# A decode step of attention and an MLP: engine programs written on their own semaphores, with each token's head outputs placed once

## The chip, the cores and the metric

The kernel runs on one core of a Trainium2 chip. A core has five engines that run their own instruction streams: TensorE (PE; its weight loads are listed as PEld), VectorE (DVE), ScalarE (ACT), GpSimd (POOL) and SyncE (SP), and 16 DMA engines that move data between the device memory and the on-chip memory SBUF. Engines wait for each other on semaphores. The metric is the device time in microseconds; lower is better.

## The reference, cut to what matters

Two tokens (B = 2) go through a layer norm; attention reads a cache of 8192 keys and values for each of 32 heads; an MLP makes a gate.

```python
xn = _layernorm(x)                                    # (2, 1, 512)
q = (xn @ wq).reshape(B, 1, 32, 128)                  # and heads in front
scores = einsum("bhqd,bhkd->bhqk", q, k_cache) * 128 ** -0.5
p = softmax(scores)
o = einsum("bhqk,bhkd->bhqd", p, v_cache)
s = o.reshape(B, 1, 4096) @ wo                        # (2, 1, 512)
g = silu(gelu(_layernorm(xn) @ w1 + b1) @ w2 + b2)
return x + s * g
```

All data are float32. Each of `k_cache` and `v_cache` has 268 MB; `wq` and `wo` have 8.4 MB each, `w1` and `w2` 2.8 MB each. Every byte is read once.

## The kernel before

The work is written in Bass under the Tile framework, which hands out buffers and sets the semaphores; the order of each engine's instructions is written out by hand (`manual_schedule`).

Two heads (U = 2) of one token make a turn; there are N = 32 turns, 16 for each token. In a turn one tile of keys and one of values, 8.4 MB each, is loaded. A tile lies with 64 of its rows (partitions) for each head, and 128 keys of 128 elements in each row. SP issues all the large loads. There are two buffers for keys (`kpool`) and one for values (`vpool`); at the start the key buffers hold `wq` and the first keys, and the value buffer (`boot`) the weights and small tensors of the MLP; at the end `wo` takes the value buffer.

Before the loop: layer norms, the MLP with its gate (`mlp`), then `project_q`, which makes the queries of all heads. `queries(k)` spreads four turns' queries over the partitions, with two products on PE and a copy on ACT; it is called once before the loop and then in every fourth turn.

In turn n the loop at L393 puts down:

- `scores_mul` (L317): DVE multiplies the keys by the query, in two halves, in place;
- between the halves `max_dve` (L335) and `exps` of the turn before: the negated maximum of each head goes through PE (L346) and ACT (L348) to all partitions, ACT makes the exponentials (L354) in `PZ` and their sums, and puts the sums in `ZR` (L357);
- `weighted` of the turn before (L369): 32 products of `PZ` with the values add up in `po`, each on one of four groups of 32 partitions; PE spends two instructions on each float32 product;
- `load_v(n)`, which needs the value buffer and so those products at their end;
- `scores_sum` (L322): DVE sums the products over the 128 elements; `max_rows` (L326) and the transposition `max_pe` (L330);
- `place` of the turn before, and `load_k(n + 2)`, which needs the key buffer that this turn has read. In the turn before the last, the last values are loaded into a key buffer, in halves.

Two turns make a group (G = 2). They share `po`; there are two of those and two `PZ`. In the second turn of a group `weighted` copies `po` to SBUF (L375) and four products turn it (L378) so that the elements lie along the partitions; `place` spreads the result on DVE over a window of `Z` (L386), and a product with a shifted view of `Z` adds it to `OA` at the rows of these heads (L390). The sums go the same way, from `ZR` (L360). `OA` is set to zero by a product at the start (L162).

After the loop, `wo` is loaded in five pieces as soon as the value buffer is free (L67), the last turn's products follow, DVE divides `OA` by the sums (L435, L437), PE multiplies by the pieces of `wo` (L442, L451, L456), DVE applies the gate (L459, L460), and two small DMAs write the output (L463). At L486 the framework ends the program: SP waits on the semaphores, the engines drain and meet, POOL clears the semaphores, and the engines meet again.

Of the kernel before, what the change touches and what calls it, by code (L numbers as in the profile page):

```python
# [1 line left out]

# [16 lines left out]
@with_exitstack  # L19
def decode_kernel(ctx: ExitStack, tc: tile.TileContext, x, kc, vc, wq, wo, w1, b1, w2, b2, out):  # L20
    nc = tc.nc
# [10 lines left out]
    G = 2  # L32
# [10 lines left out]
    ZP = P - G * UP  # L43
# [8 lines left out]
    consts = ctx.enter_context(tc.tile_pool(name="consts", bufs=1))  # L52
    kpool = ctx.enter_context(tc.tile_pool(name="kpool", bufs=2))
    vpool = ctx.enter_context(tc.tile_pool(name="vpool", bufs=1))
    small = ctx.enter_context(tc.tile_pool(name="small", bufs=2))
    ps_c = ctx.enter_context(tc.tile_pool(name="ps_c", bufs=1, space=bass.MemoryType.PSUM))
    ps_s = ctx.enter_context(tc.tile_pool(name="ps_s", bufs=4, space=bass.MemoryType.PSUM))
    ctx.enter_context(tc.manual_schedule())


    K, V = {}, {}
    kf = kc.rearrange("b h s d -> (b h s d)").rearrange("(n p j d) -> n p j d", p=P, j=KP, d=DH)
    vf = vc.rearrange("b h s d -> (b h s d)").rearrange("(n p j d) -> n p j d", p=P, j=KP, d=DH)

    def load(dst, src, cuts):
        for a, e in zip(cuts, cuts[1:]):
            nc.sync.dma_start(dst[:, a:e], src[:, a:e])  # L67

    def load_k(n, cuts=(0, KP)):
        K[n] = kpool.tile([P, KP, DH], F32, tag="k", name=f"k{n}")  # L70
        load(K[n], kf[n], cuts)

    def load_v(n, cuts=(0, KP), pool=vpool, tag="v"):
        V[n] = pool.tile([P, KP, DH], F32, tag=tag, name=f"v{n}")
        load(V[n], vf[n], cuts)

    HALVES = (0, KP // 2, KP)
# [5 lines left out]
    wq_sb = kpool.tile([P, ND, H * DH], F32, tag="k", name="wq_sb")  # L83
    boot = vpool.tile([P, KP * DH], F32, tag="v", name="boot")
    used = [0]

    def take(p, n, base=0, at=None):

        if at is None:
            at = used[0]  # L90
            used[0] += n
            assert used[0] <= KP * DH
        return boot[base:base + p, at:at + n]

    w1_sb = take(P, ND * F).rearrange("p (c f) -> p c f", f=F)
    w2_sb = take(P, WB * P)

    at = used[0]
    take(P, F + D)
    x_sb, xn, y = (take(B, D, 0, at + D * i) for i in range(3))  # L100
    b1_sb = take(1, F, R, at)
    b2_sb = take(1, D, R, at + F)
    h_row = take(B, WR * P, 2 * R, at).rearrange("b (r p) -> b r p", p=P)
    h_nat = take(B, WB * R + WM * (QT - 1), 3 * R, at)
    hs = take(P, WM * QT * QT * B).rearrange("p (a c j b) -> p a c j b", c=QT, j=QT, b=B)
    fold = take(P, QT * P).rearrange("p (c m) -> p c m", m=P)
    g_sb = take(P, 512)
    z = take(P, P)
    th = take(P, P)


    nc.sync.dma_start(w1_sb, w1.rearrange("(p c) f -> p c f", p=P))
    nc.sync.dma_start(w2_sb, w2.rearrange("f n -> (f n)").rearrange("(p e) -> p e", p=P))
    nc.sync.dma_start(wq_sb, wq.rearrange("(p c) n -> p c n", p=P))
    load_k(0, HALVES)


    eps_t = consts.tile([B, 1], F32, name="eps_t")
    nc.vector.memset(eps_t, EPS)
    warm = small.tile([B, 1], F32, tag="warm", name="warm", bufs=1)  # L120
    nc.scalar.activation(warm, eps_t, AF.Sqrt)
    nc.scalar.dma_start(x_sb, x.rearrange("b s d -> (b s) d"))
    for t, src in ((b1_sb, b1), (b2_sb, b2)):
        nc.scalar.dma_start(t.rearrange("o (k e) -> o k e", k=16), src.rearrange("(o k e) -> o k e", o=1, k=16))


    ident = consts.tile([P, P], F32, name="ident")
    make_identity(nc, ident)
    ones = consts.tile([P, B], F32, name="ones")
    nc.vector.memset(ones, 1.0)  # L130
    srow = consts.tile([1, P], F32, name="srow")
    nc.vector.memset(srow, SCALE)

    mod = consts.tile([P, R], F32, name="mod")

    blk = consts.tile([P, QT], F32, name="blk")

    cls = take(P, QT)

    half = consts.tile([P, UP], F32, name="half")  # L140
    nc.vector.memset(half, 0.0)
    for s in range(U):
        nc.vector.memset(half[HP * s:HP * (s + 1), PH * s:PH * (s + 1)], 1.0)

    Z = consts.tile([P, P + ZP], F32, name="Z")
    ZR = consts.tile([P, P + ZP], F32, name="ZR")
    nc.gpsimd.memset(Z, 0.0)
    nc.gpsimd.memset(ZR, 0.0)


    PZ = [consts.tile([P, NT, G, U, JW], F32, name=f"pz{n}") for n in range(G)]
    for t in PZ:
        nc.gpsimd.memset(t, 0.0)

    PO = [ps_c.tile([P, JW * DH], F32, name=f"po{n}") for n in range(2)]
    acc = ps_c.tile([P, P], F32, name="acc")
    OA = ps_c.tile([P, B, OC + 1], F32, name="OA")
    for t in PO + [acc]:
        nc.vector.memset(t, 0.0)

    zeros = PZ[0].rearrange("p t g s j -> p (t g s j)")
    nc.tensor.matmul(OA.rearrange("p b c -> p (b c)"), zeros[:, :P], zeros[:, :B * (OC + 1)],  # L162
                     start=True, stop=False)


    def layernorm(dst, src):
        st = take(B, nc.vector.BN_STATS_DIM)
        nc.vector.bn_stats(st, src)
        mv = take(B, nc.vector.BN_AGGR_DIM)
        nc.vector.bn_aggr(mv, st)  # L170
        sd = take(B, 2)
        nc.scalar.activation(sd[:, 0:1], mv[:, 1:2], AF.Sqrt, bias=eps_t, scale=1.0)
        nc.vector.reciprocal(sd[:, 1:2], sd[:, 0:1])
        nc.vector.tensor_scalar(dst, src, mv[:, 0:1], sd[:, 1:2], op0=ALU.subtract, op1=ALU.mult)

    def transposed(to, src, name):

        p = ps_s.tile([P, P], F32, tag="s", name=f"pt_{name}")
        for c in range(ND):
            nc.tensor.transpose(p[:, c * B:(c + 1) * B], src[:, c::ND], ident[:B, :B])  # L180
        nc.scalar.copy(to, p[:, :ND * B].rearrange("p (c b) -> p c b", b=B))


    x4 = consts.tile([P, P], F32, name="x4")
    px = ps_s.tile([P, P], F32, tag="s", name="px")
    nc.vector.memset(px, 0.0)
    for j in range(QT):
        nc.tensor.matmul(px[R * j:R * j + B, :], ident[:B, :B], x_sb[:, j * P:(j + 1) * P], start=True, stop=True)
    nc.scalar.copy(x4, px)

    layernorm(xn, x_sb)
    by_row = ident.rearrange("p (j r) -> p r j", r=R)
    nc.vector.tensor_reduce(out=mod, in_=by_row, axis=AX.X, op=ALU.add)
    nc.vector.tensor_reduce(out=blk, in_=ident.rearrange("p (j r) -> p j r", r=R), axis=AX.X, op=ALU.add)
    layernorm(y, xn)

    xnT = take(P, ND * (2 * NQ - 1) * B).rearrange("p (c b) -> p c b", c=ND)
    nc.vector.memset(xnT, 0.0)
    transposed(xnT[:, :, (NQ - 1) * B:NQ * B], xn, "xn")
    yT = take(P, ND * B).rearrange("p (c b) -> p c b", b=B)  # L200
    transposed(yT, y, "y")


    gate = consts.tile([P, P], F32, name="gate")
    for m in range(QT):
        nc.vector.tensor_reduce(out=cls[:, QT - 1 - m:QT - m], in_=ident[:, m::QT], axis=AX.X, op=ALU.add)
    nc.vector.memset(h_nat, 0.0)
    nc.gpsimd.memset(fold, 0.0)
    nc.vector.tensor_copy(fold.rearrange("p c (j r) -> p c j r", r=R)[:, :, :, :B],
                          mod.rearrange("p (c j b) -> p c j b", j=QT, b=B))  # L210

    def mlp():

        for f in range(0, F, 512):
            w = min(512, F - f)
            ph = ps_s.tile([P, 512], F32, tag="s", name=f"ph{f}")
            for c in range(ND):
                nc.tensor.matmul(ph[:B, :w], yT[:, c, :], w1_sb[:, c, f:f + w], start=(c == 0), stop=False)  # L218
            nc.tensor.matmul(ph[:B, :w], ones[R:R + 1, :B], b1_sb[:, f:f + w], start=False, stop=True)  # L219
            nc.scalar.copy(h_nat[:, 1 + f:1 + f + w], ph[:B, :w])  # L220

        for m in range(QT):
            nc.vector.tensor_copy(  # L223
                h_row[:, :, m::QT],
                h_nat[:, WM * m:WM * m + WB * R].rearrange("b (k e) -> b e k", e=WB)[:, :WR, :])
        ph = ps_s.tile([P, P], F32, tag="s", name="ph")
        for r in range(WR):
            nc.tensor.transpose(ph[:, r * B:(r + 1) * B], h_row[:, r, :], ident[2 * R:2 * R + B, 2 * R:2 * R + B])  # L228

# [46 lines left out]
    def project_q():  # L276
# [11 lines left out]
        nc.scalar.copy(q_nat, p)  # L288

    Q = {}  # L290

    def queries(k):

        b, e = divmod(k, HH // NB)
# [196 lines left out]
```

## Time and profile before

| | |
|---|---|
| median of 3 runs | 1305.62 us (1305.46 to 1305.83) |
| the profiled execution | 1305.79 us |
| its span, first to last instruction | 1303.8 us |
| DVE busy | 1132.3 us |
| PE busy | 408.2 us |
| ACT busy | 68.4 us |
| moved by DMA | 559.67 MB, 429 GB/s over the span |

The page divides the span into 40 slices and gives, for each engine and for the DMA engines, the busy share of a slice in tenths. The chain of work that ended last is followed back from the last instruction, at each step to what released it. In the timeline, a row has the start in us, the duration in us, the engine (with a `q` for the engine's queue, where it issues a DMA), the line, the operation and the tensors, how many instructions stand in the row, and in brackets how long the engine was idle before and what ended that.

### The profile page before, as it was taken

The page shows a single profiled execution, that of the slowest core. Times are in us where ns is not written, and L with a number is a line of the kernel's source. Part 1 is how long each engine was busy: PE and PEld are TensorE (multiplying, and loading weights), DVE is VectorE, ACT ScalarE, POOL GpSimd, SP SyncE. Part 2 cuts the span into 40 slices and gives each one's busy share as a digit, 9 for nine tenths or more (in the row PEclk, how much of TensorE's full clock was granted, in tenths as well). Part 3 has the DMA queues.
Part 4 walks back from the last instruction along what each step waited for, and adds up shares of the span by engine and source line. Part 5 has one row for each costly group of instructions (what it writes and reads, how often), then busy time and mean ns, then how long its engine had stood idle before and what let it go on. Part 6 is the DMA issues. An engine that isn't in the chain of part 4 may idle for free.

```text
span 1303.8 us, 6086 instructions
## 1 busy us (share of the span) xinstructions
PE 408.2 (31%) x2638; PEld 128.0 (10%) x2638; DVE 1132.3 (87%) x258; ACT 68.4 (5%) x234; POOL 2.6 (0%) x11
## 2 busy tenths in 40 slices
PE   5312333312233321323321333321323332233326
PEld 1100101001010100101000010100101010010102
DVE  3599989988889988888988888988888998888990
ACT  1000000000000000000000000000000000000000
POOL 0000000000000000000000000000000000000000
PEclk9756666556666655666655666655666665666667
DMA  9999999999999999999999999999999999999997
GB/s 409 439 420 445 424 443 426 439 426 441 424 439 426 441 426 433 434 433 436 429 438 430 431 431 434 433 433 434 431 436 431 437 424 443 424 438 429 432 426 321
DMA packets 10849, 559.67 MB, mean 429 GB/s; under 512 B 1212, under 2 KB 1220, under 8 KB 1480
## 3 DMA queue, kind: packets, MB, share of 16 engines
q1 hardware_dynamic: 10808, 559.29, 99.3%
q8 instruction: 20, 0.33, 0.1%
q14 instruction: 5, 0.04, 0.0%
q10 hardware_dynamic: 16, 0.01, 0.0%
HBM read 559.30 MB, written 0.00 MB: 429 GB/s over the span
## 4 chain that ended last, share of the span: by engine, by line
DMA 75%; PE 24%; issue 0%; ACT 0%; DVE 0%; SPq 0%
DMA v<-in_A_v_cache_dram 72%; PE po L369 22%; DMA wo_sb<-in_A_wo_dram 2%; PE ph L218 1%; DMA boot<-in_B_w_dram 1%; PE po L284 1%; PE pw L252 0%; PE po L442 0%; PE ph L219 0%; DVE boot L223 0%; PE acc L451 0%; ACT L236 0%; PE pgate L258 0%; PE ph L228 0%; SPq L67 0%
## 5 line engine op out<-in xcount | busy, mean ns | idle before, releaser
L317 DVE TENSOR_TENSOR k<-k,q 128x8192 f32<-128x8192 f32 x64 | 555.6, 8681 | 112.6 <-DMA k<-in_A_k_cache_dram 104.5
L322 DVE TENSOR_REDUCE sc<-k 128x64 f32<-128x8192 f32 x64 | 552.3, 8665 | 0.0
L369 PE MATMUL po<-v,pz 128*16 128x512 f32 x2048 | 292.1, 735 | 254.7 <-DMA v<-in_A_v_cache_dram 254.7
L346 PE MATMUL pn<-nm,srow 1*128 1x2 f32 x64 | 18.4, 355 | 362.6 <-DVE nm L335 362.6
L369 PEld LDWEIGHTS po<-v,pz 128*16 128x16 f32 x2048 | 65.2, 113 | 466.0 <-issue 353.1
L330 PE MATMUL pm<-ident,mx 128*1 128x128 f32 x32 | 11.8, 369 | 219.1 <-DVE mx L326 185.4
L346 PEld LDWEIGHTS pn<-nm,srow 1*128 1x128 f32 x64 | 15.7, 303 | 369.8 <-DVE nm L335 369.8
L348 ACT COPY bias<-pn 128x2 f32<-128x2 f32 x32 | 5.1, 161 | 862.4 <-PE pn L346 862.4
L330 PEld LDWEIGHTS pm<-ident,mx 128*1 128x1 f32 x32 | 2.5, 79 | 235.6 <-issue 137.7
L354 ACT ACTIVATE pz<-sc,bias 64x128 f32<-64x128 f32 x64 | 25.6, 399 | 1.5
L375 ACT COPY o<-po 128x512 f32<-128x512 f32 x16 | 9.4, 585 | 268.2 <-PE po L369 268.2
L378 PE MATMUL pt<-mod,o 128*128 128x4 f32 x128 | 16.9, 255 | 11.4 <-ACT o L375 11.4
L378 PEld LDWEIGHTS pt<-mod,o 128*128 128x128 f32 x128 | 15.5, 191 | 26.2 <-ACT o L375 26.2
L360 PE MATMUL OA<-ones,ZR 128*128 128x1 f32 x32 | 9.4, 363 | 25.8 <-ACT ZR L357 25.8
L299 PE MATMUL pb<-q_nat,ident 128*64 128x512 f32 x32 | 14.9, 1030 | 0.7 <-ACT q_nat L288 0.7
L386 DVE TENSOR_TENSOR Z<-blk,pt 128x16 f32<-128x16 f32 x16 | 2.6, 161 | 13.4 <-PE pt L378 13.4
L223 DVE COPY boot<-boot 2x384 f32<-2x384 f32 x4 | 1.8, 499 | 13.5 <-ACT boot L220 13.5
L354 ACT ACTIVATION_READ_ACCUMULATOR pz<-sc,bias 64x1 f32 x64 | 11.8, 184 | 0.0
L218 PE MATMUL ph<-boot 128*2 128x512 f32 (+1 forms) x24 | 11.5, 630 | 0.6 <-DMA boot<-in_B_w_dram 0.6
L459 DVE TENSOR_TENSOR gate<-acc,gate 128x128 f32<-128x128 f32 x1 | 0.3, 292 | 12.7 <-PE acc L451 12.7
L360 PEld LDWEIGHTS OA<-ones,ZR 128*128 128x128 f32 x32 | 8.0, 312 | 27.2 <-ACT ZR L357 27.2
L326 DVE TENSOR_REDUCE mx<-sc 128x1 f32<-128x128 f32 x32 | 9.2, 286 | 1.1
(88 smaller groups left out, 104.7 us busy)
## 6 DMA issues: line engine op xcount, KB each, us to landing
k<-in_A_k_cache_dram SPq DMA_DIRECT2D x4, 4096.0 KB, 37.8
v<-in_A_v_cache_dram SPq DMA_DIRECT2D x2, 4096.0 KB, 42.6
boot<-in_B_w_dram SPq DMA_DIRECT2D x2, 2752.0 KB, 12.6
wo_sb<-in_A_wo_dram SPq DMA_DIRECT2D x1, 4096.0 KB
wo_sb<-in_A_wo_dram SPq DMA_DIRECT2D x1, 2560.0 KB
wo_sb<-in_A_wo_dram SPq DMA_DIRECT2D x1, 1024.0 KB
wo_sb<-in_A_wo_dram SPq DMA_DIRECT2D x2, 256.0 KB, 29.0
v<-in_A_v_cache_dram SPq DMA_DIRECT2D x31, 30.0
```

The source lines that it names most:

```text
L218: nc.tensor.matmul(ph[:B, :w], yT[:, c, :], w1_sb[:, c, f:f + w], start=(c == 0), stop=False)
L284: nc.tensor.matmul(p[R * j:R * j + NQ * B, :].rearrange("m (h d) -> m h d", d=DH), xnT[:, c, a:a + NQ * B], w[:, h:h + NB, j % U, :], star ...
L299: nc.tensor.matmul(p[HP * s:HP * (s + 1), :], ident[:, a:a + 1].to_broadcast([P, HP]), q_nat, start=True, stop=True)
L317: nc.vector.tensor_tensor(out=k, in0=k, in1=qb, op=ALU.mult)
L322: nc.vector.tensor_reduce(out=SC[n][:, a:e], in_=K[n][:, a:e, :], axis=AX.X, op=ALU.add)
L330: nc.tensor.transpose(p[:1, :], MX[n], ident)
L346: nc.tensor.matmul(p[:, :U], srow, MX.pop(n), start=True, stop=True)
L354: nc.scalar.activation(PZ[g][r, :, g, s, :], sc[r], AF.Exp, bias=bias[r, s:s + 1], scale=SCALE, accum_out=rs[r])
L360: nc.tensor.matmul(OA[:, b, OC:], ZR[:, a:a + P], ones[:, :1], start=False, stop=False)
L369: nc.tensor.matmul(po[R * j:R * j + G * U * JW, :], PZ[g][:, t].rearrange("p g s j -> p (g s j)"), v[:, t * JW:(t + 1) * JW, :].rearrange( ...
L375: nc.scalar.copy(o4, po)
L378: nc.tensor.matmul(PT[n][:, :G * U], o4[:, i * DH:(i + 1) * DH], mod[:, i:G * U * JW:JW], start=(i == 0), stop=(i == JW - 1))
```

## The change

The Tile framework goes. A class `Plan` takes each instruction with the names of what it reads and writes, works out what it has to wait for, and emits each engine's program with one semaphore for each engine and one for each kind of DMA. PE's instructions are emitted one after the other, each with fixed addresses (`LOOP = False`; the class could emit a loop instead). The program ends when SP has waited for the two output DMAs and cleared the semaphores.

```diff
+LOOP = False
+class Plan:
+    def op(self, eng, fn, r=(), w=(), over=(), it=None, dma=None):
...
+        def after(d, war):
+            if d.dma is None and dma is None and d.eng == eng and (eng == "pe" or war):
+                return
...
+    def emit(self, loops):
...
+        def put(o, waits):
+            e = self.eng[o.eng]
+            for k, v in waits:
+                e.wait_ge(sems[k], v)
+            i = o.fn()
+            if o.dma is not None:
+                i.then_inc(sems[("dma", o.dma)], 16)
+            elif o.tell or o.eng != "pe":
+                i.then_inc(sems[o.eng], 1)
...
+        for k in ends:
+            nc.sync.wait_ge(sems[k], told[k])
+        nc.sync.sem_clear(range(first, last + 1))
+        pe = [o for o in self.ops if o.eng == "pe"]
...
+        if not loops:
+            for o in pe:
+                put(o, order(o.waits))
+            return
```

Buffers have fixed places: two for keys, one for values, one each of `PZ`, `PO`, `O4`, `mx`, `nm`, `bias`, `rs`, two of `sc`, and one `Q` for the queries of all turns. The set-up memsets stand in another order, and `wide` has a PSUM bank of its own, set to zero at the start.

The queries of all 32 turns are spread before the loop:

```diff
-    project_q()
-    queries(0)
...
-        if (n + 1) % NB == 0 and n + 1 < N:
-            queries((n + 1) // NB)
...
+    for k in range(N // NB):
...
+        for s in range(U):
+            a = R * (U * g + s) + B * i + b
+            pe(lambda p=p, s=s, a=a: matmul(p[HP * s:HP * (s + 1), :], ident[:, a:a + 1].to_broadcast([P, HP]), q_nat,
+                                            start=True, stop=True), ["ident", "o4"], [kp])
+        act(lambda p=p, k=k: nc.scalar.copy(Q[:, k * NB:(k + 1) * NB, :], p.rearrange("p (n d) -> p n d", d=DH)),
+            [kp], [("Q", k)])
```

The groups of two turns go: each turn has its own products into `PO`, with 8 columns of `PZ` where there were 16, and its own copy, turning products and spread (`spread`, in the place of `place`). `Z` and `ZR` have one tile for each token with the columns of all its heads, and two products for each token, after the loop, put them into `OA`:

```diff
+        act(lambda: nc.scalar.activation(ZR[b][:, UP * hp:UP * (hp + 1)], half, AF.Copy, scale=RS),
+            ["half"] + [("rs", s) for s in range(U)], [("ZR", n)])
...
+            pe(lambda t=t, j=j, v=v: matmul(PO[R * j:R * j + U * JW, :], PZ[:, t].rearrange("p s j -> p (s j)"),
+                                            v[:, t * JW:(t + 1) * JW, :].rearrange("p j d -> p (j d)"),
+                                            start=(t < QT), stop=(t + QT >= NT)),
+               keys + [("PZ", s) for s in range(U)], ["po"], it)
+        act(lambda: nc.scalar.copy(O4, PO), ["po"], ["o4"])
+        for i in range(JW):
+            pe(lambda i=i: matmul(PT[:, :U], O4[:, i * DH:(i + 1) * DH], mod[:, i:U * JW:JW],
+                                  start=(i == 0), stop=(i == JW - 1)), ["o4", "mod"], ["s0"], it)
...
+    for b in range(B):
+        own = range(HH * b, HH * (b + 1))
+        pe(lambda b=b: matmul(OA[:, b, OC:], ZR[b], ones[:, :1], start=True, stop=True),
+           ["ones"] + [("ZR", n) for n in own], ["OA"])
+        pe(lambda b=b: matmul(OA[:, b, :OC], Z[b], mod, start=True, stop=True),
+           ["mod"] + [("Z", n) for n in own], ["OA"])
```

The order of the turn's steps, the loads with their sizes and their order on SP, the MLP, the projection and the end with `wo` are as before.

More of the change, by code (lines that the diff above doesn't have):

```diff
@@ L58, in decode_kernel @@
[L58 to L71, printed above, removed]
@@ new lines, in decode_kernel @@
+    vbuf = vb.rearrange("p (j d) -> p j d", d=DH)
+    wq_sb = kb[0].rearrange("p (c n) -> p c n", c=ND)
+    wo_sb = vb.rearrange("p (c n) -> p c n", c=OC)
+    ident = sbuf("ident", [P, P])
+    ones = sbuf("ones", [P, B])
+    srow = sbuf("srow", [1, P])
+    eps_t = sbuf("eps_t", [B, 1])
+    warm = sbuf("warm", [B, 1])
+    mod = sbuf("mod", [P, R])
+    blk = sbuf("blk", [P, QT])
+    half = sbuf("half", [P, UP])
+    x4 = sbuf("x4", [P, P])
+    gate = sbuf("gate", [P, P])
+    Z = [sbuf(f"Z{b}", [P, P]) for b in range(B)]
@@ L85, in decode_kernel, with take @@
+    ZR = [sbuf(f"ZR{b}", [P, P]) for b in range(B)]
+    PZ = sbuf("PZ", [P, NT, U, JW])
+    Q = sbuf("Q", [P, N, DH])
+    SC = [sbuf(f"sc{i}", [P, KP]) for i in range(2)]
+    MX = sbuf("mx", [P, 1])
+    NM = sbuf("nm", [1, U])
+    BIAS = sbuf("bias", [P, U])
+    RS = sbuf("rs", [P, 1])
+    O4 = sbuf("o4", [P, JW * DH])
+    q_nat = O4
+    rl = sbuf("rl", [P, B])
+    on = sbuf("on", [P, B, OC])
     used = [0]
-    def take(p, n, base=0, at=None):
+    boot = []
+    def take(name, p, n, base=0, at=None):
@@ L189, in decode_kernel @@
[L189 to L200, printed above, removed]
@@ L201, in decode_kernel @@
-    transposed(yT, y, "y")
-    gate = consts.tile([P, P], F32, name="gate")
-    for m in range(QT):
[L206 to L210, printed above, removed]
+    take("rows", P, F + D)
+    x_sb, xn, y = (take(k, B, D, 0, at + D * i) for i, k in enumerate(("x", "xn", "y")))
@@ new lines, in decode_kernel, with bank, load @@
+    acc = psum("acc", [P, P])
+    wide = psum("wide", [P, D])
+    OA = psum("OA", [P, B, OC + 1])
+    scratch = [psum(f"s{i}", [P, 512]) for i in range(4)]
+    turn = [0]
+    def bank():
+        i = turn[0] % 4
+        turn[0] += 1
+        return scratch[i], f"s{i}"
+    kf = kc.rearrange("b h s d -> (b h s d)").rearrange("(n p j d) -> n p j d", p=P, j=KP, d=DH)
+    vf = vc.rearrange("b h s d -> (b h s d)").rearrange("(n p j d) -> n p j d", p=P, j=KP, d=DH)
+    M = KP // 2
+    def load(dst, src, sem, w, over=()):
+        op("sp", lambda: nc.sync.dma_start(dst, src), (), w, over=over, dma=sem)
@@ new lines, in load_k @@
+    def load_k(n, halves=False):
+        i = (n + 1) % 2
+        if halves:
+            for s in range(2):
+                load(kbuf[i][:, s * M:(s + 1) * M], kf[n][:, s * M:(s + 1) * M], f"k{i}{s}", [("kb", i, s)])
+        else:
+            load(kbuf[i], kf[n], f"k{i}", [("kb", i, s) for s in range(2)])
+    WO_PIECES = (0, 16, 26, 30, 31, 32)
+    WIDE = WO_PIECES[2]
+    load(w1_sb, w1.rearrange("(p c) f -> p c f", p=P), "w1", ["w1"])
+    load(w2_sb, w2.rearrange("f n -> (f n)").rearrange("(p e) -> p e", p=P), "w2", ["w2"])
@@ L263, in mlp @@
-        nc.scalar.copy(z, p)
-        nc.scalar.activation(th, z, AF.Tanh, scale=0.5)
-        nc.vector.scalar_tensor_tensor(th, th, 1.0, z, op0=ALU.add, op1=ALU.mult)
-        nc.vector.tensor_scalar_mul(gate, th, 0.5)
+            pe(lambda j=j: matmul(p[R * j:R * j + B, :P], ones[R:R + 1, :B], b2_sb[:, j * P:(j + 1) * P],
+                                  start=False, stop=True), ["ones", "b2"], [kp])
+        act(lambda: nc.scalar.copy(z, p[:, :P]), [kp], ["z"])
+        act(lambda: nc.scalar.activation(th, z, AF.Tanh, scale=0.5), ["z"], ["th"])
@@ L290, in decode_kernel @@
-    Q = {}
-    def queries(k):
+    for i in range(NQ):
+        for c in range(ND):
+            wv = wq_sb[:, c, :].rearrange("p (h s d) -> p h s d", s=U, d=DH)
+            a = (NQ - 1 - i) * B
+            for j in range(QT):
+                hd = NB * (GQ * i + j // U)
+                pe(lambda i=i, c=c, wv=wv, a=a, j=j, hd=hd: matmul(
+                    PO[R * j:R * j + NQ * B, :].rearrange("m (h d) -> m h d", d=DH),
+                    xnT[:, c, a:a + NQ * B], wv[:, hd:hd + NB, j % U, :],
+                    start=(i + c == 0), stop=(i == NQ - 1 and c == ND - 1)),
+                   ["xnT"] + [("kb", 0, s) for s in range(2)], ["po"])
@@ new lines, in decode_kernel @@
+    wo_r = wo.rearrange("(p c) n -> p c n", p=P)
+    for i, (a, e) in enumerate(zip(WO_PIECES, WO_PIECES[1:])):
+        load(wo_sb[:, a:e], wo_r[:, a:e], f"wo{i}", [("wo", i)], over=["vb"])
+    max_dve(N - 1)
+    exps(N - 1, None)
+    weighted(N - 1, None)
+    spread(N - 1)
+    for b in range(B):
[4 more added lines that the diff above has]
+           ["mod"] + [("Z", n) for n in own], ["OA"])
@@ L440, in decode_kernel, with piece @@
+    dve(lambda: nc.vector.reciprocal(rl, OA[:, :, OC]), ["OA"], ["rl"])
+    dve(lambda: nc.vector.tensor_tensor(out=on, in0=OA[:, :, :OC], in1=rl.unsqueeze(2).to_broadcast([P, B, OC]),
+                                        op=ALU.mult), ["OA", "rl"], ["on"])
+    def piece(c):
+        return ("wo", max(i for i, a in enumerate(WO_PIECES[:-1]) if a <= c))
     for c in range(WIDE):
         j = c % QT
-        nc.tensor.matmul(wide[R * j:R * j + B, :], on[:, :, c], wo_sb[:, c, :],
-                         start=(c < QT), stop=(c + QT >= WIDE))
@@ L444, in decode_kernel @@
-    w4 = small.tile([P, D], F32, tag="o4", name="w4", bufs=1)
-    nc.scalar.copy(w4, wide)
+        pe(lambda c=c, j=j: matmul(wide[R * j:R * j + B, :], on[:, :, c], wo_sb[:, c, :],
+                                   start=(c < QT), stop=(c + QT >= WIDE)), ["on", piece(c)], ["wide"])
+    w4 = O4
+    act(lambda: nc.scalar.copy(w4, wide), ["wide"], ["o4"])
     def rows(lo, hi):
```

534 lines of the change are left out of this document (298 added, 236 removed).

## The prediction

> **What bounds the kernel now.** I read the page first (slices, DMA queues, chain), then the timeline of one turn in the middle, then the chain in order of time, and last the timelines of both ends.
>
> ```profile
> span 1303.8 us, 6086 instructions
> ...
> PE 408.2 (31%) x2638; PEld 128.0 (10%) x2638; DVE 1132.3 (87%) x258; ACT 68.4 (5%) x234; POOL 2.6 (0%) x11
> ...
> DMA  9999999999999999999999999999999999999997
> ...
> DMA packets 10849, 559.67 MB, mean 429 GB/s; under 512 B 1212, under 2 KB 1220, under 8 KB 1480
> ...
> q1 hardware_dynamic: 10808, 559.29, 99.3%
> q8 instruction: 20, 0.33, 0.1%
> ...
> DMA 75%; PE 24%; issue 0%; ACT 0%; DVE 0%; SPq 0%
> ```
>
> The DMA engines are busy in every slice, and one queue (q1, filled by SP) takes 99.3% of their time. The chain calls 24% of the span PE's, so the next question is whether the DMA engines rest while PE works. The timeline of a turn answers it:
>
> ```profile
> 569.20 0.33 SPq L67 DMA_DIRECT2D v<-in_A_v_cache_dram  x1
> 575.91 0.33 SPq L67 DMA_DIRECT2D k<-in_A_k_cache_dram  x1
> ...
> 600.27 9.14 PE L369 MATMUL po<-v,pz 128*16 128x512 f32 x64 [7.66 <-DMA v<-in_A_v_cache_dram]
> 609.49 0.33 SPq L67 DMA_DIRECT2D v<-in_A_v_cache_dram  x1
> ...
> 615.59 0.33 SPq L67 DMA_DIRECT2D k<-in_A_k_cache_dram  x1
> ...
> 619.61 8.69 DVE L317 TENSOR_TENSOR k<-k,q 128x8192 f32<-128x8192 f32 x1 [3.65 <-DMA k<-in_A_k_cache_dram]
> ```
>
> The v issued at 569.20 is in at 600.27; the k issued behind it, at 575.91, is in at 619.6, which is 19.3 us after v. So loads are served in the order of issue, about 19.4 us for each 8.39 MB (432 GB/s). The next v is issued at 609.49, while that k has 10.1 us left to run; the next k at 615.59, with that rest and a whole v in front of it. The queue is never empty: the bound is bytes over rate. PE's 9.14 us and the DVE lie beside a running transfer. The turn has a slack of 10.1 us for the issue of v, and a step that stays inside it costs nothing.
>
> ```profile
> 95.32 9.08 PE po L369 x64
> ...
> 444.43 8.62 PE po L369 x64
> ...
> 483.25 9.67 PE po L369 x64
> ...
> 521.87 9.15 PE po L369 x64
> ...
> 1065.48 8.71 PE po L369 x64
> ...
> 1104.29 9.76 PE po L369 x64
> ...
> 1143.89 8.75 PE po L369 x64
> ...
> 1260.34 8.54 PE po L369 x64
> ```
>
> Thirty turns take 1260.34 - 95.32 = 1165.0, or 38.83 each. An undisturbed pair takes (521.87 - 444.43) / 2 = 38.72. The difference times 30 is 3.4 us, and it comes in steps: 1143.89 - 1104.29 = 39.60 against 1104.29 - 1065.48 = 38.81. So only three things can move the time: the head before the first byte, the tail after the last, and these 3.4 us.
>
> **Part by part.** *Own semaphores in the loop.* The waits for each load are the same ones (v after the last product of the turn before, k after the sum that read the buffer), so the order of loads is unchanged. A few more wait instructions on SP would have to add up to 10.1 us in a turn: nothing. If the cover were gone, each us of later issue would cost a us in each of 31 turns.
>
> *Outputs placed once per token.* Now every turn, not every other one, ends with a copy of `po`, the small transposing products and a spread on DVE.
>
> ```profile
> L317 DVE TENSOR_TENSOR k<-k,q 128x8192 f32<-128x8192 f32 x64 | 555.6, 8681 | 112.6 <-DMA k<-in_A_k_cache_dram 104.5
> ...
> L378 PE MATMUL pt<-mod,o 128*128 128x4 f32 x128 | 16.9, 255 | 11.4 <-ACT o L375 11.4
> ...
> L375 ACT COPY o<-po 128x512 f32<-128x512 f32 x16 | 9.4, 585 | 268.2 <-PE po L369 268.2
> ```
>
> That doubles L375 (16 x 0.585 = 9.4 us more on ACT) and L378 (16.9 us more on PE), and the spread is 16 more small DVE operations. In PE's order they stand behind the products with v, so the issue of the next v isn't behind them; what is, is the transposition of the next maxima, which waits for the DVE until 615.6 anyway, 6 us after the products end. DVE stands idle 104.5 us in 29 waits for k, 3.6 us a turn, which covers its extra 0.2 us. All of it is hidden; uncovered, PE's would be 0.5 us a turn. Against that, the 30 products into OA leave the loop, from beside the transfers too: no gain.
>
> *All queries ahead.* The seven later broadcasts move to before the loop, on PE and ACT alone. On PE they stand ahead of the first turn's transposition, on ACT ahead of the first exponentials. The loads of k1 and v0 wait for the projection and the MLP, which come before them as now.
>
> ```profile
> 45.26 0.33 SPq L67 DMA_DIRECT2D v<-in_A_v_cache_dram  x1
> ...
> 56.49 8.69 DVE L317 TENSOR_TENSOR k<-k,q 128x8192 f32<-128x8192 f32 x1 [0.72 <-DMA k<-in_A_k_cache_dram]
> ```
>
> Both are issued by 45.6 while k0 runs until about 56: some 10 us of slack at the head. The first DVE product needs only the first broadcast. Cost nothing. The set-up memsets change places with the same slack over them. SP's first load stays the first instruction behind the start barrier, so the first byte does not move.
>
> *The tail.* The four OA products now follow the last spread.
>
> ```profile
> 1268.90 2.23 SPq L67 DMA_DIRECT2D wo_sb<-in_A_wo_dram  x5
> ...
> 1274.59 0.59 PE L360 MATMUL OA<-ones,ZR 128*128 128x1 f32 x2 [1.61 <-ACT ZR L357]
> 1275.11 9.64 PE L369 MATMUL po<-v,pz 128*16 128x512 f32 x64
> ...
> 1286.78 0.41 PE L390 MATMUL OA<-mod,Z 128*128 128x32 f32 x2 [0.26 <-DVE Z L386]
> 1287.23 0.17 DVE L435 RECIPROCAL rl<-OA 128x2 f32<-128x2 f32 x1 [0.50 <-PE OA L390]
> 1287.43 0.22 DVE L437 TENSOR_TENSOR on<-OA,rl 128x64 f32<-128x64 f32 x1
> 1289.97 5.60 PE L442 MATMUL po<-wo_sb,on 128*2 128x512 f32 x32 [2.78 <-DMA wo_sb<-in_A_wo_dram]
> 1296.00 2.74 PE L442 MATMUL po<-wo_sb,on 128*2 128x512 f32 x20 [0.43 <-DMA wo_sb<-in_A_wo_dram]
> ...
> 1301.03 0.65 SPq L463 DMA_DIRECT2D out_dram<-gate  x1
> ```
>
> Three pairs more at 0.41 to 0.59 us are +1.2 to +1.8; they run partly under the copy and spread. The L360 pair ahead of the last products goes: 1275.11 can come 0.5 earlier. Net +0.7 to +1.3 at `on`, which is ready at 1287.65 and needed at 1289.97, when the first piece of wo is in. Slack 2.3 us: cost nothing. Uncovered, it would be at most 1.3 us. From 1296.00 on, products, gate and output are the same instructions.
>
> *The exit.*
>
> ```profile
> SPq L486 <- DMA out_dram<-gate: 1.0, 1, 1.0
> ```
> ```profile
> L486 SPq EVENT_SEMAPHORE  x8: 17/28/28, 1301.7 to 1303.8; - x8
> ...
> L486 SPq DRAIN  x3: 7/7/7, 1303.1 to 1303.4; - x3
> ...
> L486 POOLq EVENT_SEMAPHORE_RANGE_CLEAR  x1: 96/96/96, 1303.5 to 1303.5; - x1
> ```
>
> Once the output has landed, the framework's exit goes through its remaining waits, drains, meets, clears the semaphores on POOL and meets again: from SP's first drain at 1303.1 to 1303.8, 0.7 us. The change has SP wait for the two outputs and clear the semaphores itself, about 0.1 us by the 96 ns row; most of SP's eight waits, 0.2 us at 28 ns, go. Bounds: 0 (if another exit is added) to -0.9 (0.7 and 0.2, the clearing free); I take -0.7, nearer the full end because the rows show each piece that goes.
>
> *The program's size.* Behind the q8 row stand 20 fetches, some 16 KB each, on the engines that carry the loads. I take the 3.4 us above for them: a fetch holds one DMA engine up, and a load is in only when the last engine is. PE gets 128 more products and some 58 fewer, each with a weight load: about 140 instructions more on twice 2638, 20 fetches becoming 20 or 21. If each cost the mean, 3.4 / 20 = 0.17, that is +0.2. A step, 39.60 - 38.81, is 0.8. Bounds: -3.4 (all fetches miss the last engine) to +1; I take +0.1. The Trainium skill (Runtime: NRT & Kernel Launch, Instruction fetch mechanics) says that code comes in 16 KiB blocks and that crossing a boundary is "mostly hidden"; the size agrees with the q8 row, and by that rule this term is 0 and the sum -0.7. The skill (DMA: Bandwidth & Descriptors, Queues, rings and completion order) has each engine alternate between queues packet by packet, which speaks against "hidden" where the queue beside it is never empty; the steps agree with it.
>
> **Sum.** -0.7 + 0.1 = -0.6 us. The profiled execution took 1305.79 (span 1303.8 and 2.0 around it), 0.17 above the median 1305.62 of three runs; from its own time 1305.2, from the median 1305.0. I forecast 1305.0: no change that a measurement of this kernel tells from none, for which I take 0.2%, or 2.6 us.
>
> **The rivals.** *Fewer collisions, faster.* If the fetches fall on other engines and the lag vanishes, it is -3.4 - 0.7: 1301.5. For it: the lag comes in a few steps, so it depends on where fetches fall. Against it: their number stays and their kind too; only over half of the lag gone would count. 7%.
>
> *The queue runs dry, slower.* The stationary operand of L369 has 8 columns, not 16. If narrower products no longer ran four at a time on the four groups of output rows, the 64 would take 4 x 9.14 = 36.6 us. The point from which it decides is the end of the other transfer, 19.4 us after v is in. Each turn would then leave the queue empty for 17 us: 31 x 17 = +527, about 1833. Against it: L442, with 2 columns, does 20 products in 2.74 us, 0.55 for four; L369 with 16 takes 9.14 / 16 = 0.57. 2%. A milder form is an issue of v delayed by some other wait, past the 10.1 us in a few turns only, from +3 to +20 (1308 to 1325): 4%. Nothing in the diff puts a wait there.
>
> *Fetches fall worse, slower.* If all 21 held up the same engine by a step of 0.8 it would be 16.8 - 3.4 = +13.4, about 1318. The present ones do not, as 20 of them cost 3.4. 3%.
>
> *The change does not do what it says.* If an exit like the present one is still emitted, the time is 1305.7: 10%, within my forecast's bounds.
>
> **How the numbers follow.** No change (the forecast, and the exit that stays): 84%. Faster by over 0.2%: 7%, and 1% for a cause not seen. Slower by over 0.2%: 2 + 4 + 3 = 9%, less 1 for the part of the last two that stays under 2.6 us: 8%. The range goes down to the exit at -0.9 with half of the lag gone (1303.0) and up to the exit unchanged with one more step and the scatter of the runs (1306.8).
>
> **What would show it.** Right: all 40 DMA slices full, the turns at 38.7 to 38.8, v issued some 10 us before k is in, wide products still waiting for wo near 1290, the end some 0.1 us after the output lands. Wrong: a turn over 40 us, a DMA slice under 9 in the middle, products with v well over 10 us, a q8 row far from 20, or L442's counterpart waiting for `on`.

## The result, and the profile after

| | before | changed |
|---|---|---|
| median | 1305.62 us (1304.78 to 1306.78, 22 runs) | 1303.95 us (1303.37 to 1304.23, 22 runs) |
| profiled execution | 1305.79 us | 1304.13 us |
| its span | 1303.8 us | 1302.8 us |
| around the span | 1.95 us | 1.35 us |

The ratio is 0.9986, with a 95% interval of 0.998 to 0.9993: 1.67 us less, 0.13%. That is a gain clear of the noise, but one inside the 0.2% that was called no change. The forecast had 0.6 us less than before, so the gain is nearly three times that.

The page of the changed kernel, the lines that answer to those of before:

```profile
span 1302.8 us, 6084 instructions
...
PE 402.5 (31%) x2708; PEld 119.7 (9%) x2708; DVE 1132.9 (87%) x273; ACT 77.7 (6%) x250; POOL 1.4 (0%) x8
...
DMA  9999999999999999999999999999999999999997
...
q1 hardware_dynamic: 10808, 559.29, 99.4%
q8 instruction: 21, 0.34, 0.1%
```

The DMA engines are as full as they were, PE has 70 products more, ACT 9.3 us more, and one fetch of code is added. The timeline of the same turn as before:

```profile
568.74 0.33 SPq L315 DMA_DIRECT2D vb<-in_A_v_cache_dram  x1
...
575.58 0.33 SPq L315 DMA_DIRECT2D kb<-in_A_k_cache_dram  x1
...
599.81 9.11 PE L551 MATMUL po<-vb,PZ 128*8 128x512 f32 x64 [9.86 <-DMA vb<-in_A_v_cache_dram]
608.99 0.33 SPq L315 DMA_DIRECT2D vb<-in_A_v_cache_dram  x1
...
609.63 1.05 PE L558 MATMUL s<-mod,o 128*128 128x2 f32 x8 [0.71 <-ACT o L556]
615.13 0.33 SPq L315 DMA_DIRECT2D kb<-in_A_k_cache_dram  x1
...
615.48 0.37 PE L522 MATMUL s<-ident,mx 128*1 128x128 f32 x1 [4.79 <-DVE mx L520]
619.14 8.69 DVE L510 TENSOR_TENSOR kb<-kb,Q 128x8192 f32<-128x8192 f32 x1 [3.65 <-DMA kb<-in_A_k_cache_dram]
```

The products with 8 columns take 9.11 us where those with 16 took 9.14. The next v is issued at 608.99, with 10.1 us of k still to run, as before. The turning products (L558) now stand in each turn, and PE still waits 4.79 us after them for the DVE. The chain in order of time gives the turns:

```profile
95.18 8.89 PE po L551 x64
...
1064.92 8.72 PE po L551 x64
...
1104.43 9.43 PE po L551 x64
...
1143.14 8.86 PE po L551 x64
...
1259.34 8.78 PE po L551 x64
```

Thirty turns take 1164.16 us, 38.81 each (38.83 before); the turn from 1064.92 has a step (39.51), the next one has not (38.71). In the whole chain four turns have one (39.35, 39.55, 39.40 and 39.51). The tail, from the timeline:

```profile
1273.60 4.99 PE L551 MATMUL po<-kb,PZ 128*8 128x512 f32 x32 [1.38 <-ACT PZ L535]
...
1285.39 0.39 PE L609 MATMUL OA<-mod,Z 128*128 128x32 f32 x2
1285.81 0.17 DVE L611 RECIPROCAL rl<-OA 128x2 f32<-128x2 f32 x1 [0.76 <-PE OA L609]
1286.01 0.22 DVE L612 TENSOR_TENSOR on<-OA,rl 128x64 f32<-128x64 f32 x1
1289.19 5.73 PE L621 MATMUL wide<-vb,on 128*2 128x512 f32 x32 [3.42 <-DMA vb<-in_A_wo_dram]
...
1300.28 0.65 SPq L643 DMA_DIRECT2D out_dram<-gate  x1
```

`on` is ready at 1286.23, 3.0 us before wo lets PE start (2.3 before). And the exit, from the instructions of the two lines that wait and clear:

```profile
L123 SPq EVENT_SEMAPHORE  x1: 17/17/17, 1302.2 to 1302.2; - x1
```
```profile
L124 SPq EVENT_SEMAPHORE_RANGE_CLEAR  x1: 76/76/76, 1302.7 to 1302.7; - x1
```

The last output is waited for at 1302.7, and 0.08 us later the program is over. From the issue of the output to the end it takes 1302.8 - 1300.28 = 2.5 us, where it took 1303.8 - 1301.03 = 2.8. The difference in the span is thus 0.3 at the exit and 0.75 ahead of the output's issue, by one profile each; and 0.6 lies around the span. How much of this is the change and how much one execution's chance, the experiments had to say.

### The profile page after: what moved, and what is told of

The parts are those of the page before. It is cut to its first block, busy times and chain, and to the rows that moved or that the text cites. A ratio compares the mean times of both kernels' runs of the same rounds, so it can differ in the third digit from the quotient of the medians.

```text
span 1302.8 us, 6084 instructions
## 1 busy us (share of the span) xinstructions
PE 402.5 (31%) x2708; PEld 119.7 (9%) x2708; DVE 1132.9 (87%) x273; ACT 77.7 (6%) x250; POOL 1.4 (0%) x8
## 3 DMA queue, kind: packets, MB, share of 16 engines
q1 hardware_dynamic: 10808, 559.29, 99.4%
## 4 chain that ended last, share of the span: by engine, by line
DMA 74%; PE 22%; DVE 3%; another core or an unknown queue 0%; issue 0%; SPq 0%
DMA vb<-in_A_v_cache_dram 68%; PE po L551 22%; DMA kb<-in_A_k_cache_dram 3%; DMA vb<-in_A_wo_dram 2%; DVE kb L510 2%; DVE sc L516 1%; PE wide L621 0%; SPq L315 0%; PE acc L630 0%; PE s L530 0%; DVE gate L639 0%; DVE gate L640 0%; DVE mx L520 0%; PE acc L635 0%
## 5 line engine op out<-in xcount | busy, mean ns | idle before, releaser
L510 DVE TENSOR_TENSOR kb<-kb,Q 128x8192 f32<-128x8192 f32 x64 | 555.6, 8681 | 111.4 <-DMA kb<-in_A_k_cache_dram 111.4
L516 DVE TENSOR_REDUCE sc<-kb 128x64 f32<-128x8192 f32 x64 | 552.3, 8666 | 0.0
L551 PE MATMUL po<-vb,PZ 128*8 128x512 f32 x1984 | 282.5, 734 | 299.6 <-DMA vb<-in_A_v_cache_dram 299.6
L530 PE MATMUL s<-nm,srow 1*128 1x2 f32 x64 | 18.4, 355 | 368.0 <-DVE nm L525 368.0
L551 PEld LDWEIGHTS po<-vb,PZ 128*8 128x8 f32 x1984 | 54.9, 103 | 501.0 <-DMA vb<-in_A_v_cache_dram 302.2
L522 PE MATMUL s<-ident,mx 128*1 128x128 f32 x32 | 11.8, 369 | 185.2 <-DVE mx L520 185.2
L530 PEld LDWEIGHTS s<-nm,srow 1*128 1x128 f32 x64 | 15.7, 303 | 377.2 <-DVE nm L525 368.5
L558 PE MATMUL s<-mod,o 128*128 128x2 f32 x256 | 33.7, 254 | 22.9 <-ACT o L556 22.9
L558 PEld LDWEIGHTS s<-mod,o 128*128 128x128 f32 x256 | 31.0, 191 | 52.6 <-ACT o L556 52.6
L535 ACT ACTIVATE PZ<-sc,bias 64x128 f32<-64x128 f32 x64 | 25.5, 399 | 1.8
```

Source lines behind the costliest of these rows:

```text
L510: dve(lambda: nc.vector.tensor_tensor(out=k, in0=k, in1=Q[:, n].unsqueeze(1).to_broadcast([P, M, DH]), op=ALU.mult), [("kb", i, s), ("Q", ...
L516: dve(lambda: nc.vector.tensor_reduce(out=SC[n % 2][:, s * M:(s + 1) * M], in_=k, axis=AX.X, op=ALU.add), [("kb", i, s)], [("sc", n % 2, s)])
L522: pe(lambda: transpose(PM[:1, :P], MX, ident), ["mx", "ident"], ["s1"], it)
L530: pe(lambda: matmul(PN[:, :U], srow, NM, start=True, stop=True), ["srow", "nm"], ["s2"], it)
L535: act(lambda r=r, s=s: nc.scalar.activation(PZ[r, :, s, :], sc[r], AF.Exp, bias=BIAS[r, s:s + 1], scale=SCALE, accum_out=RS[r]), ["bias", ...
L551: pe(lambda t=t, j=j, v=v: matmul(PO[R * j:R * j + U * JW, :], PZ[:, t].rearrange("p s j -> p (s j)"), v[:, t * JW:(t + 1) * JW, :].rearra ...
```

## The experiments

The runs of one group share a chip and the runs of the kernel before; its median there is given. The changed kernel itself ran in none of the groups; e4, e8, e10 and e11, which came out like its 1303.95 us, stand for it.

**First group: undo one part each** (before: 1305.49 us).

*The old exit back* (e1):

```diff
-        nc.sync.sem_clear(range(first, last + 1))
...
             for o in pe:
                 put(o, order(o.waits))
+            nc.all_engine_barrier()
+            nc.gpsimd.sem_clear(range(first, last + 1))
+            nc.all_engine_barrier()
             return
```

> The changed kernel, with the exit of the kernel before put back: after the last instructions all engines meet, POOL clears the semaphores, all engines meet again. Theory A (the exit makes the gain that isn't in the loop): the span grows by the 0.7 to 0.9 us that the old exit took behind the landing of the output, and the time around the span goes from 1.3 us back to about 1.9, since all engines are held to the end again; in all +0.7 to +1.5, about 1305. Rival B (the time around the span comes from something else, the head or the buffers): the span grows by 0.7 to 0.9, and the time around it stays at 1.3. Rival C (the exit is worth nothing): 1304.0 as the changed kernel.

Measured: 1305.33 us (1304.73 to 1305.65), a ratio to before of 1.0 (0.9991 to 1.0009). The profiled execution has a span of 1303.9 and 1.79 us around it. So Theory A holds: with the old exit the changed kernel is as slow as the kernel before, and about 1.4 us of the gain (1305.33 against 1303.9 to 1304.0 of e4 and e8) is the exit's. Its rows:

```profile
L130 SPq DRAIN  x1: 112/112/112, 1303.1 to 1303.1; - x1
```
```profile
L132 PEldq EVENT_SEMAPHORE  x1: 51/51/51, 1303.8 to 1303.8; - x1
```

The 0.7 us from SP's drain to the last engine's release are those that the prediction read; the 0.4 around the span are not in any row. One thing weakens the 1.4: from the issue of the output to the end of the span, e1's profile takes 3.1 us, where the kernel before and e3 take 2.8. The exit put back is thus some 0.3 us longer than the one that went, in one profile of it, and the exit of the kernel before may be worth 1.1 to 1.4 us.

*The kernel before, its buffers moved* (e3):

```diff
-    nc = _bacc.Bacc("TRN2", target_bir_lowering=False, num_devices=1)
+    nc = _bacc.Bacc("TRN2", target_bir_lowering=False, num_devices=1, dynamic_dma_scratch_size=4096)
```

> The kernel before, with 4096 bytes in each partition set aside at the bottom of SBUF for descriptors, as the changed kernel has it, and not the default; every buffer moves down. Theory A (the place of the buffers makes the pace): the 64 KB packets go from 2.4224 us in the mean to the 2.4210 of the changed kernel, and the time falls by 0.5 to 0.8 us against the kernel before. Rival B (the pace differs from chip to chip or run to run): no difference from the kernel before on the same chip, within 0.3 us, and the packets are as long as in that run's neighbours.

Measured: 1305.16 us, a ratio of 0.9999 (0.999 to 1.0008). The place of the buffers makes no difference that this run can tell: Rival B. The packets of 64 KB took 2.4239 us in the mean in its profile, against 2.4243 of the kernel before and 2.4227 of the changed one (the expectation had put these last two at 2.4224 and 2.4210, too low). Its profile issues the output at 1300.50, as that of e4 does (1300.50) and between the 1301.03 and 1300.28 above; e1's issues it at 1300.77. So the 0.75 us ahead of the output's issue are no more than executions of these kernels differ among themselves; what makes them differ stays open.

*The queries in the loop again* (e4), and *the outputs placed in every turn again* (e8):

```diff
+    def queries(k):
...
+        if (n + 1) % NB == 0 and n + 1 < N:
+            queries((n + 1) // NB)
```

> The changed kernel, with the queries of four turns each spread inside the loop again, at the place they had before. Theory A (the work lies beside the transfers): within 0.3 us of the changed kernel, about 1304.0. Rival B (the queries in the loop held the DVE up or the transfers): +0.5 us and more, up to the 1.67 of the whole change.

```diff
-            out=Z[b][:, UP * hp:UP * (hp + 1)].rearrange("p (s r) -> p s r", r=PH),
+            out=Z[:, ZP:P].rearrange("p (s r) -> p s r", r=PH),
...
+        a = ZP - UP * hp
+        pe(lambda: matmul(OA[:, b, :OC], Z[:, a:a + P], mod, start=False, stop=(n == N - 1)), ["mod", "Z"], ["OA"])
```

> The changed kernel, with the outputs and the sums put into OA in every turn again, through one shifted window each, and not once per token: 60 more products in the loop, 4 fewer behind it, some 250 more instructions on TensorE in all. Theory A (hidden in the loop and covered by the wait for wo at the end): within 0.3 us of the changed kernel; one more fetch of code may add up to 0.5. Rival B (placing once per token makes the gain): +0.5 to +1.7 us.

Measured: 1303.99 us (1303.43 to 1304.14) and 1303.90 us (1303.24 to 1304.48). Both are as the changed kernel (e8 with 22 fetches of code for 21): neither part is worth anything that shows, as Theory A had it.

**Second group: the exit taken apart, the slack, the code** (before: 1305.53 us).

*One meeting behind the landing of the outputs* (e9), and *one meeting before SP waits for them* (e10):

```diff
-        nc.sync.sem_clear(range(first, last + 1))
...
             for o in pe:
                 put(o, order(o.waits))
+            nc.all_engine_barrier()
+            nc.sync.sem_clear(range(first, last + 1))
             return
```

> The changed kernel; when SP has waited for the outputs, all engines meet once, and then SP clears the semaphores. Theory A (the part of the gain around the span comes from the other engines being done before the end): the span grows by 0.3 to 0.6 us and the time around it goes from 1.35 to about 1.8, in all about 1304.8. Rival B (the time around the span comes from POOL's clearing or the second meeting): the span grows by 0.3 to 0.6, and the time around it stays at 1.35, in all about 1304.4.

```diff
-        for k in ends:
-            nc.sync.wait_ge(sems[k], told[k])
-        nc.sync.sem_clear(range(first, last + 1))
...
             for o in pe:
                 put(o, order(o.waits))
+            nc.all_engine_barrier()
+            for k in ends:
+                nc.sync.wait_ge(sems[k], told[k])
+            nc.sync.sem_clear(range(first, last + 1))
             return
```

> The changed kernel; all engines meet once, but before SP waits for the outputs, so that the meeting lies under their landing. Theory A (only engines that are held behind the landing cost time): as the changed kernel within 0.2 us, 1304.0, with 1.35 us around the span. Rival B (a meeting costs wherever it stands, by its drains): +0.3 to +0.8, 1304.3 to 1304.8.

Measured: e9 1304.70 us, with 1.71 us around the profiled span; e10 1303.73 us (1302.91 to 1304.02), with 1.33. The same meeting costs 1.0 us behind the landing and nothing before it. Each kernel whose other engines are done before the end has 1.33 to 1.36 us around the span (nine profiles of this study), each that holds them to the end has 1.71 to 2.06 (four). The medians over all runs agree: 1.33 to 1.36 and 1.71 to 1.91. So that part goes with holding all engines, and POOL's clearing or the second meeting isn't needed for it: Theory A twice. What is done around the span, no row shows.

*The next values issued 6 us later* (e5), and in the third group *3 us* (e11) and *15 us later* (e6); the number of idle copies is 10, 5 and 24:

```diff
         act(lambda: nc.scalar.copy(O4, PO), ["po"], ["o4"])
+        for _ in range(10 if n < N - 2 else 0):
+            act(lambda: nc.scalar.copy(LATE, PO), ["po", "vb"], ["late"])
```

> The changed kernel; behind the products with the values ScalarE makes ten idle copies of 0.6 us in a turn, for which the load of the next values waits: it is issued some 6 us later in 29 turns. Theory A (the queue has 10 us of slack there, served in the order of issue): as the changed kernel within 0.5 us, 1303.5 to 1304.5. Rival B (TensorE's products lie on the chain, as the chain of waits has them with 22% of the span): 29 x 6 = +174 us, about 1478.

> The changed kernel with five idle copies of ScalarE in place of ten: the load of the next values is issued some 3 us later in 29 turns, with some 6.5 us left to run in front of it. Theory A (the handover costs only when the next load is issued less than some 4 us ahead): 1304.0, within 0.5 us. Rival B (the loss grows in proportion to the delay): half of the 19 us that ten copies cost, +9, about 1313. Rival C (the copies themselves disturb the transfers): half of the 19 us as well, and slow packets while the copies run, not at the handover.

> The changed kernel with 24 idle copies of ScalarE in a turn: the load of the next values is issued some 15 us later, 4.5 us after the transfer in front of it has ended. Theory A (the queue runs dry): DMA engines idle for 5 to 7 us in each of 29 turns, with the start of a transfer added, 1304 + 145 to 200 = 1450 to 1505. Rival B (the chain of waits): 29 x 15 = 435 us more, about 1739.

Measured: 3 us later 1303.96 us, nothing; 6 us later 1323.01 us (1317.27 to 1325.86, five runs), +19; 15 us later 1542.55 us (two runs), +239. The products of PE, 22% of the span by the chain of waits, are not on the path: +174 and +435 did not come. The slack is there, but Theory A of e5 was wrong: not all of the 10 us is free. How much of k is left when v is issued is read from the timeline, here for two turns of e5:

```profile
581.51 0.33 SPq L316 DMA_DIRECT2D vb<-in_A_v_cache_dram  x1
...
585.77 8.69 DVE L511 TENSOR_TENSOR kb<-kb,Q 128x8192 f32<-128x8192 f32 x1 [3.85 <-DMA kb<-in_A_k_cache_dram]
...
605.14 9.57 PE L552 MATMUL po<-vb,PZ 128*8 128x512 f32 x64 [9.86 <-DMA vb<-in_A_v_cache_dram]
```
```profile
699.88 0.33 SPq L316 DMA_DIRECT2D vb<-in_A_v_cache_dram  x1
...
703.28 8.69 DVE L511 TENSOR_TENSOR kb<-kb,Q 128x8192 f32<-128x8192 f32 x1 [4.17 <-DMA kb<-in_A_k_cache_dram]
...
724.61 9.57 PE L552 MATMUL po<-vb,PZ 128*8 128x512 f32 x64 [11.81 <-DMA vb<-in_A_v_cache_dram]
```

and of e11:

```profile
612.13 0.33 SPq L316 DMA_DIRECT2D vb<-in_A_v_cache_dram  x1
...
619.17 8.69 DVE L511 TENSOR_TENSOR kb<-kb,Q 128x8192 f32<-128x8192 f32 x1 [3.65 <-DMA kb<-in_A_k_cache_dram]
```

In e11, 7.0 us of k are left in this turn, 5.8 to 7.4 in the others but the first and the last, and nothing is lost. In e5 the rest differs from turn to turn. In the first turn shown 4.3 us are left, and v is in 19.4 us after k, as without the delay; in the second 3.4 us are left, and v is in 21.3 us after k. Over the 27 turns whose v is issued from 150.51 to 1171.59, the nine with over 4 us left take 38.7 to 38.8 us from k to k, except one of 39.2; the 18 with 2.7 to 3.9 us left take 39.5 in the mean and up to 40.7. So the loss, 0.65 us a turn in the mean (19 / 29), isn't in proportion to the delay: it comes where less than some 4 us are left, as Theory A of e11 had it. All these turns make the same ten copies, so the copies alone do not make it either.

More of the loss is slower packets than idle time: the row of the loads' queue in e5's page,

```profile
q1 hardware_dynamic: 10808, 559.29, 98.9%
```

is 98.9% of a span of 1320.3 us, 1306 us, where the changed kernel has 99.4% of 1302.8, 1295: the same packets took 11 us longer, of the 17.5 us by which the span grew. In the records of the packets, a packet of 64 KB takes 2.42 us in the mean; where the one load goes over into the next, many take 3 to 4 us in most of the turns that lose. Why they do was not settled. In e6 the queue runs dry:

```profile
583.00:588.00 5.00, 0.00 (x0) 0.00 (x0) 4.70 (x1) 4.48 (x8) 0.00 (x0) 0.50 0.00 0
```

This window (us, busy times of the engines, clock, DMA share, GB/s) has no byte moved in 5 us. A turn costs 239 / 29 = 8.2 us, more than the 5 to 7 expected: in this turn 4.4 from k being in (583.30, where the DVE starts) to the issue of v (587.72), 2.5 more than 19.4 us until v is in (609.67), and 1.0 by which this k itself came in later than 19.4 us after the v in front of it (562.93 to 583.30). With the 38.8 us of two transfers without a delay they make this turn's 46.7 (562.93 to 609.67).

*Twice the code* (e7) and, in the third group (before: 1305.18 us), *TensorE's turns as a loop* (e2):

```diff
+        for _ in range(40):
+            pe(lambda: matmul(scratch[3][:B, :1], ones, ones[:, :1], start=True, stop=True), ["ones"], ["s3"])
```

> The changed kernel; TensorE makes 40 products of one column more in each turn, into a bank that nothing reads, while it waits for the DVE: some 5000 instructions more, 40 fetches of code where there were 21. Theory A (each fetch holds up one of eight DMA engines in turn by 0.5 to 1.0 us, and the load is in when the last engine is): 5 hits on the worst engine for 3, +1 to +2 us, 1305.0 to 1306.0. Rival B (fetches are hidden): 1304.0, within 0.3 us.

```diff
-LOOP = False
+LOOP = True
```

> The changed kernel with TensorE's 31 turns as a loop, the waits counted up in a register, and not unrolled. Theory A (each fetch of code costs some 0.18 us, by 41 fetches for 21): if the loop is fetched once, 5 or 6 fetches are left and the time falls by about 2.8 us, to 1301.2. Rival B (the loop's code is fetched again in each turn): 30 to 60 fetches and +2 to +7 us. Rival C (fetches fall into a loss that something else sets): 1304.0.

Measured: e7 1307.77 us (1307.42 to 1308.07), twice the upper end of the expected rise; e2 1300.78 us (1300.6 to 1301.3), a ratio to before of 0.9967 (0.9954 to 0.9979). The rows of the code queue on the two pages, e7's first:

```profile
q8 instruction: 41, 0.67, 0.2%
```
```profile
q8 instruction: 4, 0.07, 0.0%
```

And the first and the last of the 30 turns in the chain of each, e7's first:

```profile
95.09 9.09 PE po L553 x64
...
1263.12 8.77 PE po L553 x64
```
```profile
95.47 8.80 PE po L551 x64
...
1256.83 8.39 PE po L551 x64
```

| fetches | median us | us a turn |
|---|---|---|
| 4 (e2) | 1300.78 | 38.71 |
| 21 (e10, e11 and the changed kernel) | 1303.73 to 1303.96 | 38.81 (changed kernel) |
| 41 (e7) | 1307.77 | 38.93 |

From 4 to 21 fetches a fetch costs (1303.96 - 1300.78) / 17 = 0.19 us, from 21 to 41 it costs (1307.77 - 1303.73) / 20 = 0.20. The loop, with the same products, runs at 38.71 us a turn, which is the undisturbed pace; of the steps one small one is left (38.92). In the profiles alone, its thirty turns take 2.8 us less than those of the changed kernel. Code fetches make the lag, Theory A of e2. e7 also keeps PE busier, and e2 also counts its waits in a register; but each lacks what the other adds, and both give the same price.

The records of the packets show the fetches at work. While the loads move packets of 64 KB, each fetch (16 KB, 1.06 us in the mean) is followed, just as it ends, by one such packet that takes 2.88 to 2.97 us in place of 2.42: 17 of 17 in the kernel before, 17 of 17 in the changed one, one of one in e2, 36 of 36 in e7. Few other packets are as long (two, one, one and eight). The long ones repeat in a row of eight (2.91, 2.92, 2.93, 2.89, 2.89, 2.90, 2.97, 2.97), in the kernel before, the changed one and e7, which fits eight DMA engines that are hit in turn; no row names the engines. That picture gave e7 the right direction and half the size or less; the mean of 0.17 did better. e2 is the fastest version: 1300.78 us, 3.2 us under the changed kernel's 1303.95 and 4.4 under the kernel before on its chip.

## Why the prediction was right or wrong, point by point

*The bound.* Right. The loads are served in the order of issue, the queue is always filled, and PE's 9.1 us lie beside it (e5, e11, e6 against the chain). Wrong was the sentence that a step inside the 10.1 us costs nothing: it holds up to 3 us (e11), and at 6 us (e5) a turn lost 0.65 in the mean, nearly all of it in turns with less than 4 us left.

*Own semaphores in the loop, outputs, queries.* Right: 0, as undone in e4 and e8. The turning products end 4.8 us before the DVE has the maxima.

*The tail.* Right in its result, wrong in its sign: the net at `on` was put at +0.7 to +1.3, but `on` came 1.4 us earlier, and 0.6 us earlier relative to wo, which itself came 0.8 earlier in this execution. The start of the last products was read well: 1273.60 against 1275.11 is 0.7 earlier relative to wo, where 0.5 was expected, since PE goes on when `PZ` is ready and no longer waits for the sums to be in ZR. The three pairs more were priced too high, at +1.2 to +1.8: from the copy of the last products (1283.16, and 1284.83 before) to `on` it takes 3.07 us, where it took 2.82, because each pair starts 0.22 us behind the one in front (1284.72, 1284.94, 1285.16, 1285.39). It is covered either way.

*The exit.* This is the term that was mis-sized: -0.7, with -0.9 as the bound, against 1.4 measured in e1, or 1.1 if the 0.3 us by which e1's exit is longer are taken off. Its part inside the span was about right, if a little high: e1's spans are 0.8 to 0.9 us longer than those of e4 and e8 (medians 1303.5 against 1302.7 and 1302.6), with those 0.3 in them. The failing step is where the 2.0 us around the span were carried over as a constant. They went to 1.35, with only SP left at the end (e9 against e10).

*The program's size.* Right in kind, and shown by e2 and e7: the 3.4 us are the fetches'. One fetch more costs 0.19, near the mean that the prediction worked out as 0.17, not the 0.1 taken. Of the two rules of the Trainium skill that stood against each other, "mostly hidden" (Runtime: NRT & Kernel Launch, Instruction fetch mechanics) does not hold for this kernel, whose DMA queue is never empty. The Trainium skill's packet-by-packet alternation of the queues (DMA: Bandwidth & Descriptors, Queues, rings and completion order) is in keeping with the one long packet behind each fetch, though no row shows the alternation itself.

*The sum.* With the terms as measured it is -1.4 + 0.2 = -1.2 (-0.9 with the exit at 1.1), against -1.67 by 22 runs each and about -1.5 on the chip of the first group. The first lies in the interval of the ratio (0.9 to 2.6 us less) and the second at its edge, so the rest, 0.3 to 0.8, can't be told from chance; it was not traced further. That the time fell into the range (1303.0 to 1306.8) is in part luck: the low end had been stretched for half of the lag to vanish. The lag stayed, 38.81 us a turn after 38.83, and what used the room was the time around the span, which the sum did not have.

*The rivals.* No queue ran dry, and the fetches fell neither more kindly nor worse: 17 long packets before, 17 after. Over 4, 21 and 41 fetches the cost goes by their number, which speaks against a lag that vanishes by chance. The exit did not stay. The signs that were named came: full DMA slices, turns of 38.8 us, v issued 10.1 us before k is in, the products with wo waiting for it at 1289.19, the end 0.08 us after the output's landing was seen.

## What to carry to other kernels

In a kernel whose DMA queue is full from end to end, look for what else uses the DMA engines: unrolled code cost 3.2 us here, more than every rearrangement of the compute gained, and a loop for one engine took it back. At the end let only the engine that waits for the output live on; whatever must meet, meets before that wait. And read a chain of waits with the queue's order in mind: a step that it names may have 10 us of slack behind it, of which some 6 were free here.

## What the runs showed of the hardware that was not expected

- A fetch of 16 KB of code cost 0.19 to 0.20 us beside a full DMA queue, the same per fetch from 4 to 41 of them, and one 64 KB packet behind each took 2.88 to 2.97 us in place of 2.42.
- Time around the span went with the engines that are held to the end: 1.33 to 1.36 us when only SP is left, 1.71 to 2.06 when all are.
- Where a load was issued 2.7 to 3.9 us before the one in front of it ended, packets at the change-over took 3 to 4 us in place of 2.42 in most turns, and a turn lost 0.8 us in the mean; with over 4 us left, eight turns of nine lost next to nothing, and with 5.8 to 7.4 (e11) the run lost nothing.
